# Attention and gated MLP on one core: softmax without row maxima, a range check with a branch, and a new order of steps

## The chip, the cores and the metric

The kernel runs on one core of a Trainium2 chip. The metric is the device time of one execution in microseconds (us); the median of several runs counts. TensorE is called PE here, VectorE DVE, ScalarE ACT, GpSimd POOL, and SP is SyncE, whose queue only issues DMAs.

## The reference, cut to what matters

```python
q_n, k_n = rmsnorm(q, g_q), rmsnorm(k, g_k)          # q, k, v: 8 batches x 12 heads x 448 x 64, float32
scores = matmul(q_n, k_n.T) / 8
scores = scores - max(scores, axis=-1)
attn = exp(scores)
attn = attn / (sum(attn, axis=-1) + 1e-09)
x = matmul(attn, v)                                   # heads side by side: 8 x 448 x 768
h = maximum(x @ w_in, 0)                              # w_in 768 x 1024
conv_out = 3-tap convolution of h along the sequence, per channel
out = (h * sigmoid(conv_out)) @ w_out                 # w_out 1024 x 768
```

Taking any number off a row of scores before exp leaves `attn` as it is, but for the 1e-09 and for rounding.

## The kernel before, in words

**Pairs.** The work is cut into 48 pairs `n` of heads, six to a batch. Each pair has seven tiles `j` of 128 query rows (2 heads x 448 rows). Pairs 0 to 9 are computed in float32 (`whole`), pairs 10 to 47 with each float32 operand split into a high and a low float16 half, and three matmuls in place of one.

**Attention of a pair.** `load_k`, `load_q` and `v_load` bring in the data. `square`, `square_sum` and nine small steps `rsqrt` make the factors of the norm, and `apply_rms` (two multiplications, L276 where a helper records them) applies them. PE or a DMA turns q and k (`qk_transpose`, `q_turn`), and ACT or DVE copies them out of PSUM (`qk_hi`, tile `kT` times the gain `G`, tile `qT`). `scores` (L856) fills two PSUM banks for a group of two tiles. `soft_max` (L864) takes the negative row maxima of both banks in one reduction on DVE. `soft_exp` (L876) on ACT reads a bank, adds that maximum as its bias, and writes exp to tile `e` with the row sum (`rsum`) beside it. A bank is free again when exp has read it. Pairs from 10 on then split `e` into tile `ph`: `p_hi` (L264, a cast) and `p_lo` (L276, a subtraction in two instructions); `p_turn` (L896) is a DMA transpose of `ph` into `PT` on SP's queue. There are six places for `ph`. Pairs 0 to 9 turn `e` on PE (`p_transpose`, L904) and copy it (`p_evac`). `sum_add`, `sum_step` and the steps after them turn the row sums into a row of reciprocals, `pv` (L996) multiplies with v, and `x_scale`, `x_hi`, `x_lo` leave x in two halves.

**MLP of a batch.** `in_part` (L1080) multiplies x with `wi`, `in_relu`, `in_conv`, `in_tanh`, `in_gate`, `in_hi` and `in_lo` make the gated tile `gring` (`g`), `out_part` (L1149) multiplies it with `wo`, `out_evac` and `out_store` write the result.

**Weights.** They come as 64-bit numbers. `convert` turns them into float32 with three integer steps on DVE (L391, L395, L399), then they are scaled and split.

**Order.** All steps are put into a list `plan`; the string `ORDER` says, four characters for a step, in which order they are issued, on which engine each stands, and which PSUM bank it takes. Each engine runs its instructions in that order and waits at each for its inputs. A POOL step that would share a port with DVE waits for the last DVE step ahead of it in the order (the "shared port" rule).

The lines at which the order is read and the lines of the softmax:

```python
        a, b, e, z = (DIGITS.index(x) for x in ORDER[4 * i : 4 * i + 4])
        fn, args = plan[len(DIGITS) * a + b]
        step, e = (fn.__name__, *args), ("PE", "DVE", "ACT", "POOL", "SP")[e]
        ...
        nc.vector.tensor_reduce(st, banks[:, i : i + 2, :S], axis=AX.X, op=ALU.max, negate=True)
        ...
        nc.scalar.activation(
            new("e", (n, j), [P, S], F32), held["s", (n, j)][:, :S], AF.Exp, bias=shift(n, j),
            accum_out=old("rsum", n)[:, c : c + 1],
        )
```

Of the kernel before, what the change touches and what calls it, by code (L numbers as in the profile page):

```python
# [20 lines left out]
    "$2&!$4$!$3&!$y&!$z&!$?$!${$!$P&!!!#!!6&!$5#!$6#!$7#!$8%!$9%!%;&!!7&!$:%!$|#!$@#!$A%!$Q#!%y&!$;#!"  # L21
    "$B#!$}#!$C#!!0&!$~#!%!%!$<%!%*$!%+#!!8&!!9&!%##!$D#!%f&!%,#!$=#!$E#!%-#!!:#!%.#!%$#!$F#!%/#!!;#!"
    "%0#!!?#!$G#!%1#!$>#!$H#!%%#!%2#!$I#!$M%!%g&!!1#!$J%!%<#!%z#!!<#!%3#!!@#!$N!#$O$!$K!+$L$!$R!8!D#!"
    "%4#!!A#!!B$!!>&!!C&!!E#!$T!L$V!b!I#!&D&!&E&!!F#!!H&!!J#!%&%!!G$!$S#!$U#!&N&!%(%!%h$!%i#!$X$!$W#!"
    "$[$!%8%!%9!#%)%!$Y!+%5%!!S#!!N#!!K#!!M&!$_$!%:$!$c$!!O#!$]!#!T#!$Z$!!P#!!U#!!R&!$a!$$^$!$b$!%6!("
    "%7$!&F$!$f$!(0&!(c&!!Q$!!W&!&G#!!X#!%=!B%>#!%j%!%k#!!Y#!!^#!$d!+$g!#$e$!!Z#!$i$!!_#!$j!$!]&!%l#!"
    "%m%!%n%!!V$!$l$!$o%!$h$!%?!V%@#!$k$!%o%!%p%!&O#!%q%!$p#!%A!l%B#!!L$!$q#!!a#!!c&!%E$!%r#!!=$!%v%!"
    "&y&!(1#!$r&!&z&!%C!.%D#!%s%!(W&!(d#!$m!%%F!&!d#!!h#!%H$!![$!!e#!(e#!!f#!!i#!!l#!$n$!%I!(%G$!#(&!"
    "%K$!!j#!!m#!%w!%#)&!%J$!!p#!!n#!%t!&!q#!%N$!&K%!%Q$!%x$!$s&!)F&!%u$!%L!+%O!*%{!V$t&!%|#!%}!B%T$!"
    "%W$!%M$!%P$!%R!#%U!$(X&!%X!+%S$!(f!*(g#!%~#!%Z%!!g$!&H%!!#%!!b$!!r#!%[#!#/#!#*#!%V$!#0#!%]#!%Y$!"  # L30
    "!k$!&$$!#+#!$u!##1#!#,#!!o$!&($!&+$!&%!$&&$!&L!*&M$!&I!+%^&!&J$!&.$!&!!V&##!#.&!&)!$&*$!&P!l&R!B"
    ")y&!*Y&!$v#!&Q#!&{$!%_&!(Y%!&,!$$w%!$x%!#3&!&/!#(Z#!&|#!&}%!&1$!&4$!)G#!&2!(#4#!!/%!&-$!&7$!&~#!"
    "%b!)(!%!&S#!(#%!&:%!#5#!($#!!s$!!t#!&;#!)z#!(%%!(&%!&X$!#-$!&0$!&3$!%a&!)3&!&5!$&6$!#6#!((#!#9#!"
    "&[$!()#!(*%!([%!&8!*&9$!&Y!+&_$!&T!.&]!(&Z$!&^$!&U#!&a!%&b$!!u!*!v#!(-%!&c$!%c#!(_%!&V!L(+!+&d!%"
    "&W#!(,#!#:#!!x$!!y#!&f$!!%%!&e$!(.!#(/$!&i$!(a!)(b$!#8&!#>#!&l$!#;#!!z$!#?#!(]!+(^#!&<#!)4&!)5$!"
# [186 lines left out]
WHOLE = 10  # L222
# [22 lines left out]
def tile_attention_moe(ctx: ExitStack, tc, q, k, v, g_q, g_k, w_in, conv_w, w_out, out):  # L245
# [366 lines left out]
    def duo(n):  # L612

        return (n, 1) if n < 2 else (n - n % 2, 2)
# [725 lines left out]
```

## Time and profile before

| | |
|---|---|
| median of 3 runs | 806.55 us (805.41 to 807.5) |
| the profiled execution's own time | 807.84 us |
| its span, first to last instruction | 806.1 us |
| mean granted clock of PE | 0.994 |
| busy: PE, DVE, ACT, POOL | 763.9, 701.9, 665.8, 464.4 us |

The profile is of one execution. Busy time of an engine is the time in which at least one of its instructions runs; matmuls are pipelined, so several run at once and the next may start before the last has ended. SP only issues, so it has no busy time in the tables; what its queue does is read from its timeline and its waits. Four stretches are used below: up to the first exp (22.5 us), pairs 0 to 9 (to 153.5 us, the first exp of pair 10), pairs 10 to 45 (to 707.6 us, the first exp of pair 46), and the rest.

### The profile page before, as it was taken

Reading aid. Unit: us, or ns where it says so; the run is one execution under the profiler, and the core shown is the slowest. Engines: PE = TensorE matmul, PEld = TensorE weight load, DVE = VectorE, ACT = ScalarE, POOL = GpSimd, SP = SyncE. Lnnn points to the kernel's source line nnn. Section 1 sums busy time; section 2 is a strip of 40 time slices with the busy share of each in tenths; the row PEclk is TensorE's granted clock in tenths of the full one; section 3 lists DMA queues with packets and bytes.
Section 4 is the critical chain, followed back from the end, with each engine's and each line's share of the span. In section 5 each row is a group of like instructions: output and inputs, shape, how many; then the busy total and the mean of one; then the engine's idle time right before and its main releaser. Section 6 shows DMA issues by size and latency. Waiting matters only on the chain.

```text
span 806.1 us, 16603 instructions
## 1 busy us (share of the span) xinstructions
PE 763.9 (95%) x5278; PEld 401.9 (50%) x5278; DVE 701.9 (87%) x1469; ACT 665.8 (83%) x1568; POOL 464.4 (58%) x727
## 2 busy tenths in 40 slices
PE   1799999999999999999999999999899999999998
PEld 1355555544545554455445554455444554455554
DVE  5999999999889899999889999999889899986640
ACT  2979999998989799999889988999889788973221
POOL 2346555675668557595567654864578655882110
PEclk9989999999999999999999999999999999999999
DMA  8884653299999999999998999999999999887002
GB/s 227 241 199 141 150 142 99 58 192 189 179 194 168 176 184 192 173 186 179 191 199 148 197 192 179 171 180 183 190 188 159 182 192 164 142 136 149 5 1 78
DMA packets 353420, 130.84 MB, mean 162 GB/s; under 512 B 295708, under 2 KB 349748, under 8 KB 353332
## 3 DMA queue, kind: packets, MB, share of 16 engines
q1 hardware_dynamic: 344436, 121.50, 80.1%
q10 hardware_dynamic: 8896, 8.28, 3.9%
q8 instruction: 41, 0.67, 0.4%
q14 instruction: 47, 0.39, 0.1%
HBM read 48.20 MB, written 11.80 MB: 74 GB/s over the span
## 4 chain that ended last, share of the span: by engine, by line
PE 51%; ACT 17%; DMA 11%; DVE 11%; issue 6%; POOL 3%; SPq 0%; ACTq 0%; DVEq 0%; POOLq 0%
PE bank L1149 20%; PE bank L1080 13%; PE bank L856 7%; PE bank L996 7%; DMA PT<-ph 6%; ACT ph L264 2%; PE bank L904 2%; DMA PT<-PT 2%; ACT PT L264 2%; PE bank L673 2%; DMA v<-in_v_dram 1%; ACT bank L1088 1%; POOL ph L276 1%; DMA qT<-qkf 1%; ACT sq L592 1%
## 5 line engine op out<-in xcount | busy, mean ns | idle before, releaser
L1080 PE MATMUL bank<-x,wi 128*128 128x448 f16 x1152 | 230.2, 354 | 3.3 <-ACT e_(37_2_7498 L876 1.1
L1149 PE MATMUL bank<-wo,gring 128*128 128x384 f16 (+1 forms) x1056 | 197.4, 327 | 0.8 <-ACT e_(13_3_2355 L876 0.4
L1080 PEld LDWEIGHTS <-wi 128*128 128x128 f16 x1152 | 110.6, 98 | 112.1 <-issue 17.2
L856 PE MATMUL bank<-kT,qT 64*128 64x448 f16 (+3 forms) x1072 | 137.7, 393 | 9.8 <-DMA qT<-qkf 1.5
L1149 PEld LDWEIGHTS <-gring 128*128 128x128 f16 (+1 forms) x1056 | 100.8, 99 | 72.0 <-issue 19.2
L276 POOL TENSOR_TENSOR sq<-qkf,st 112x512 f32<-112x512 f32 (+1 forms) x66 | 67.9, 1043 | 63.3 <-issue 24.0
L996 PE MATMUL bank<-PT,vp 128*64 128x448 f16 x836 | 87.0, 355 | 2.2 <-DMA PT<-ph 0.8
L996 PEld LDWEIGHTS <-vp 128*64 128x64 f16 x836 | 46.3, 109 | 40.0 <-issue 13.8
L856 PEld LDWEIGHTS <-qT 64*128 64x128 f16 (+1 forms) x912 | 34.2, 97 | 63.4 <-issue 43.4
L592 ACT ACTIVATE sq<-qkf 128x1024 f32<-128x1024 f32 (+2 forms) x49 | 50.2, 1030 | 5.7 <-DMA qkf<-in_k_dram 3.8
L673 PE MATMUL bank<-ident,sq 128*128 128x128 f32 (+1 forms) x232 | 36.1, 284 | 19.7 <-POOL sq L276 19.1
L601 DVE TENSOR_REDUCE st<-sq 128x16 f32<-128x1024 f32 x38 | 45.7, 1211 | 4.3 <-ACT sq L592 4.2
L276 POOL TENSOR_TENSOR x<-x,x 128x448 f16<-128x448 f32 x31 | 32.1, 1037 | 25.9 <-ACT x L264 6.9
L1149 PE MATMUL bank<-wo,wi 128*128 128x384 f16 (+1 forms) x192 | 46.9, 326 | 0.0
L276 POOL TENSOR_TENSOR qkf<-sq,qkf 112x512 f16<-112x512 f32 x33 | 38.2, 1160 | 13.1 <-DVE ph L276 4.6
L673 PEld LDWEIGHTS bank<-ident,sq 128*128 128x128 f32 (+1 forms) x232 | 26.8, 146 | 33.0 <-POOL sq L276 21.8
L1088 ACT ACTIVATE bank<-bank 128x448 f32<-128x448 f32 x53 | 28.4, 538 | 14.8 <-PE bank L1080 14.4
L264 ACT COPY PT<-bank 112x512 f32<-112x512 f32 x64 | 36.5, 616 | 3.4 <-PE bank L904 3.4
L1149 PE MATMUL bank<-wo,carry 128*64 128x384 f16 x192 | 34.5, 328 | 0.0
L766 DVE TENSOR_REDUCE vacc<-v 128x1 f32<-128x512 f32 (+1 forms) x48 | 32.1, 675 | 0.7 <-DMA v<-in_v_dram 0.4
L996 PE MATMUL bank<-PT,v 112*64 112x448 f32 x160 | 32.3, 545 | 0.0
L1149 PE MATMUL bank<-wo 128*128 128x384 f16 (+1 forms) x96 | 31.3, 326 | 0.0
(2065 smaller groups left out, 1894.5 us busy)
## 6 DMA issues: line engine op xcount, KB each, us to landing
qkf<-in_q_dram SPq DMA_DIRECT2D x18, 448.0 KB
wo<-in_moe_w_in_dram SPq DMA_DIRECT2D x12, 512.0 KB
gring<-in_moe_w_out_dram SPq DMA_DIRECT2D x16, 384.0 KB
qkf<-in_k_dram SPq DMA_DIRECT2D x18, 256.0 KB
v<-in_v_dram SPq DMA_DIRECT2D x15, 256.0 KB
qkf<-in_k_dram SPq DMA_DIRECT2D x17, 192.0 KB
v<-in_v_dram SPq DMA_DIRECT2D x15, 192.0 KB
PT<-ph SPq DMA_TRANSPOSE x178
```

Of the source, the lines that this page charges most:

```text
L264: (nc.scalar.copy if e == "ACT" else elementwise(e).tensor_copy)(dst, src)
L276: elementwise(e).tensor_tensor(dst, a, b, op=op)
L592: nc.scalar.activation(sq, x, AF.Square)
L601: nc.vector.tensor_reduce(st, sq, axis=AX.X, op=ALU.add)
L673: nc.tensor.transpose(ps[:, t * w : (t + 1) * w], x[:, t], ident[:w, :w])
L766: nc.vector.tensor_reduce(keyed(n, old("vacc", b))[:, i : i + 1], keyed(n, old("v", n)).rearrange("p h t d -> p (h t d)"), axis=AX.X, op=A ...
L856: nc.tensor.matmul(ps[u][o, :S], lhs, rhs, start=(i == 0), stop=(whole(m) or i == 2),)
L904: nc.tensor.transpose(ps[:w, kt * P : (kt + 1) * P], e[:, kt * w : (kt + 1) * w], ident)
L996: nc.tensor.matmul(ps[HALF[h], :S], lhs, pt[:, k, h * S : (h + 1) * S], start=(i == 0 and j == 0), stop=(i == pvs(n)[-1] and j == NB - 1),)
L1080: nc.tensor.matmul(ps[:, :S], wi[:, wl, c, fc * P : (fc + 1) * P], old("x", b * NP + c)[:, xl], start=(i == 0), stop=(i == 3 * NP - 1),)
L1088: nc.scalar.activation(ps, ps, AF.Relu, scale=2.0 ** -24)
L1149: nc.tensor.matmul(ps[p0 : p0 + m, :NO2], g, wo[:, wl, fc, half * NO2 : (half + 1) * NO2], start=(i == 0), stop=(i == 3 * NFC - 1),)
```

## The change

`soft_max` is no longer issued: exp has the constant -4 as its bias. The row sums of all pairs go into a tile `raw`; at the end of each batch DVE takes their largest and smallest (`sum_range`), and after the last batch `sum_check` makes one number of them, which is above 1 if a sum exceeds 6e4 or falls below 1. PE and DVE bring it to one place (`range_turn`, `range_top`), every engine loads it into a register, and a branch skips a second, general program, which computes everything again with row maxima. The general program stands behind the branch in every engine's instructions. `ORDER` is new as a whole, with its engines and banks.

```diff
@@ soft_exp and what it reads
-        i, j = sorted(where["s", x] for x in members(n, g))
-        assert j == i + 1
-        nc.vector.tensor_reduce(st, banks[:, i : i + 2, :S], axis=AX.X, op=ALU.max, negate=True)
+        for u, x in enumerate(members(n, g)):
+            nc.vector.tensor_reduce(
+                st[:, u : u + 1], held["s", x][:, :S], axis=AX.X, op=ALU.max, negate=True
+            )
 
     def shift(n, j):
 
-        a, b = members(*group(n, j))
-        c = 1 if where["s", (n, j)] > where["s", a if b == (n, j) else b] else 0
-        return old("sst", group(n, j))[:, c : c + 1]
+        if not general:
+            return lift
...
+    def raw_sums(n):
+
+        return raw[:, n // NP % 2, n % NP]
 
     def soft_exp(n, j):
-        if j == 0:
-            fixed("rsum", n, sums)
         c = slot(n, j)
         nc.scalar.activation(
             new("e", (n, j), [P, S], F32), held["s", (n, j)][:, :S], AF.Exp, bias=shift(n, j),
-            accum_out=old("rsum", n)[:, c : c + 1],
+            accum_out=raw_sums(n)[:, c : c + 1],
         )
 
+    def sum_range(b):
+        x = raw[:, b % 2].rearrange("p n j -> p (n j)")
+        nc.vector.tensor_reduce(span[:, 0, b : b + 1], x, axis=AX.X, op=ALU.max)
+        nc.vector.tensor_reduce(span[:, 1, b : b + 1], x, axis=AX.X, op=ALU.min)
+
+    def sum_check():
+        high, low = top[:, 0:1], top[:, 1:2]
+        nc.vector.tensor_reduce(high, span[:, 0], axis=AX.X, op=ALU.max)
+        nc.vector.tensor_reduce(low, span[:, 1], axis=AX.X, op=ALU.min)
+        nc.vector.tensor_scalar(low, low, 1e-30, None, op0=ALU.max)
+        nc.vector.reciprocal(low, low)
+        nc.vector.scalar_tensor_tensor(
+            high, high, 1.0 / MOST, low, op0=ALU.mult, op1=ALU.max
+        )
+        nc.vector.tensor_scalar(high, high, 1e30, None, op0=ALU.min)
+
+    def range_turn():
+        max_turn("range", top[:, 0:1])
+
+    def range_top():
+        all_max(top[:, 2:3], "range")
@@ plan_attention
             at(scores, n, g)
-            at(soft_max, n, g)
...
+        if n % NP == NP - 1:
+            at(sum_range, n // NP)
+        if n == NPAIR - 1:
+            at(sum_check)
+            at(range_turn)
+            at(range_top)
@@ at the end
+    flag = nc.values_load(top[0:1, 2:3].bitcast(I32), min_val=0, max_val=0x7FFFFFFF)
+    with tc.If(flag > 0x3F800000):
+        general = True
+        with tc.manual_schedule():
+            run_general()
@@ ORDER, the first of 199 lines (now 193)
-    "$2&!$4$!$3&!$y&!$z&!$?$!${$!$P&!!!#!!6&!$5#!$6#!$7#!$8%!$9%!%;&!!7&!$:%!$|#!$@#!$A%!$Q#!%y&!$;#!"
+    "$2&!$3&!$v&!$w&!$4$!$?$!$x$!%&$!!6&!!!#!$5#!$6#!%^&!$7#!!7&!!0&!!8&!$@#!$P&!$8%!$9%!$y#!$:#!%(#!"
...
```

What the new order puts where is seen in the instructions of each engine. Counted over the whole order: DVE loses 168 maxima and takes 55 more low halves of p (`p_lo`, 92 to 147), 22 more multiplications of `apply_rms` (30 to 52), 14 more copies `PT<-bank` (6 to 20), 12 more casts of `p_hi`, 12 more `gring` subtractions and some 60 smaller moves; POOL goes from 174 to 119 low halves of p and from 66 to 44 of `apply_rms`; ACT gives up 75 instructions. PE's instructions are the same but for one, and so are SP's transposes.

**The start.** SP's queue before, after the first loads of k and q (`gqk` are the two gains, `wo` the place into which the words of `w_in` come first):

```order
L568 DMA qkf_77<-in_q_dram 112x2x128 x2
L554 DMA v<-in_v_dram 112x2x256
L430 DMA wo_84<-in_moe_w_in_dram 128x1024
L554 DMA v<-in_v_dram 112x2x256
L430 DMA wo_84<-in_moe_w_in_dram 128x1024
L554 DMA v<-in_v_dram 112x2x256
L1196 DMA gqk<-in_g_q_dram 64x1 x2
L1196 DMA gqk<-in_g_k_dram 64x1 x2
L430 DMA wo_84<-in_moe_w_in_dram 128x1024 x2
```

SP's queue now, at the same place:

```order
L576 DMA qkf_77<-in_q_dram 112x2x128 x2
L438 DMA wo_84<-in_moe_w_in_dram 128x1024
L562 DMA qkf_78<-in_k_dram 112x2x256
L438 DMA wo_84<-in_moe_w_in_dram 128x1024
L1236 DMA gqk<-in_g_q_dram 64x1 x2
L1236 DMA gqk<-in_g_k_dram 64x1 x2
```

Three loads of v now stand behind the gains, and one load of k ahead of them.

DVE before, around the step of `convert` (L391) that needs the second load of weights, up to the gain `G` (`st` holds the factors of the norm, `st_95` those of pair 0):

```order
L395 SCALAR_TENSOR_TENSOR wi_83<-wo_84,wi_83 128x512
L629 SCALAR_TENSOR_TENSOR st_103<-st_103 112x8
L391 TENSOR_SCALAR wi_83<-wo_84 128x512
L644 TENSOR_TENSOR st_95<-st_95 112x8
L642 TENSOR_TENSOR st_103<-st_103 112x8
L629 SCALAR_TENSOR_TENSOR st_95<-st_95 112x8 x2
L642 TENSOR_TENSOR st_103<-st_103 112x8
L644 TENSOR_TENSOR st_103<-st_103 112x8
L629 SCALAR_TENSOR_TENSOR st_95<-st_95 112x8
L1199 TENSOR_TENSOR G<-gqk 128x1
L1200 TENSOR_SCALAR G<-G 128x1
```

DVE now, to the same two instructions of `G`:

```order
L650 TENSOR_TENSOR st_107<-st_107 112x8
L637 SCALAR_TENSOR_TENSOR st_103<-st_103 112x8
L279 TENSOR_TENSOR sq_104<-qkf_76,st_103 112x2x4x64
L637 SCALAR_TENSOR_TENSOR st_103<-st_103 112x8
L399 TENSOR_SCALAR wi_83<-wo_84 128x512
L279 TENSOR_TENSOR sq_104<-qkf_76,st_103 112x2x4x64
L399 TENSOR_SCALAR wi_83<-wo_84 128x512
L1239 TENSOR_TENSOR G<-gqk 128x1
L1240 TENSOR_SCALAR G<-G 128x1
```

The two multiplications of `apply_rms` of pair 0 (`sq_104<-qkf_76,st_103`), which POOL did before, are now on DVE, and both stand ahead of the second L399, which is the L391 of before.

**The middle.** DVE before, at the first tiles of pair 30 (`sst` are maxima, `ph` the halves of p, `sq` with `st` is `apply_rms`):

```order
L276 TENSOR_TENSOR ph_74<-e_(30_0_5984,ph_74 128x384
L276 TENSOR_TENSOR ph_74<-e_(30_0_5984,ph_74 128x64
L629 SCALAR_TENSOR_TENSOR st_5870<-st_5870 128x32
L864 TENSOR_REDUCE sst_(30_1_6029<-bank 128x2
L276 TENSOR_TENSOR sq_5874<-qkf_76,st_5870 112x2x4x64
L276 TENSOR_TENSOR ph_75<-e_(30_1_5989,ph_75 128x384
L276 TENSOR_TENSOR ph_75<-e_(30_1_5989,ph_75 128x64
L276 TENSOR_TENSOR sq_5871<-qkf_76,st_5870 112x2x4x64
L864 TENSOR_REDUCE sst_(30_2_6043<-bank 128x2
L276 TENSOR_TENSOR x_6020<-x_28_6006,x_6020 128x448
```

DVE now, at the same tiles:

```order
L279 TENSOR_TENSOR ph_74<-e_(30_0_5802,ph_74 128x384
L279 TENSOR_TENSOR ph_74<-e_(30_0_5802,ph_74 128x64
L279 TENSOR_TENSOR sq_5655<-qkf_76,st_5622 112x2x4x64
L279 TENSOR_TENSOR sq_5623<-qkf_76,st_5622 112x2x4x64
L279 TENSOR_TENSOR ph_75<-e_(30_1_5823,ph_75 128x384
L279 TENSOR_TENSOR ph_75<-e_(30_1_5823,ph_75 128x64
L279 TENSOR_TENSOR PT_70<-e_(30_2_5850,PT_70 128x384
L279 TENSOR_TENSOR PT_70<-e_(30_2_5850,PT_70 128x64
L1108 TENSOR_TENSOR vsc_5661<-vsc_5661,wsc 128x1
L1111 COPY vsc_4251<-vsc_5661 64x1
```

The maxima between the other steps are gone, and the low half of tile (30, 2), which stood on POOL, is on DVE.

**The end.** PE's last instructions before (`wo` holds the weights; the rest of `wi` and `wo` also serves as places of the gated tile):

```order
L1149 MATMUL bank<-wo_84,wi_83 128x384
L1149 LDWEIGHTS wi_83
L1149 MATMUL bank<-wo_84,wi_83 128x384
L1149 LDWEIGHTS wo_84
L1149 MATMUL bank<-wo_84 128x384
L1336 UNCONDITIONAL_BRANCH
```

PE's last instructions of the first program now:

```order
L1189 MATMUL bank<-wo_84,wi_83 128x384
L1189 LDWEIGHTS wo_84
L1189 MATMUL bank<-wo_84 128x384
L378 MATMUL bank<-ident,top 128x128
L1395 TENSOR_LOAD top
L1396 COMPARE_AND_BRANCH
```

The turn of the check (`top`), a load of it into a register and the branch stand behind the last matmul, and on each other engine the same load and branch stand behind its last step; DVE reduces `top` ahead of them.

## Rows read from the trace of the kernel before

**Rows 1.** The page: busy time of each engine, share of the span, instructions.
```profile
PE 763.9 (95%) x5278; PEld 401.9 (50%) x5278; DVE 701.9 (87%) x1469; ACT 665.8 (83%) x1568; POOL 464.4 (58%) x727
```

**Rows 2.** Four stretches: busy us by engine, granted clock, DMA share, GB/s.
```profile
0.00:22.50 22.50, 6.09 (x20) 3.19 (x20) 14.37 (x53) 7.34 (x13) 4.83 (x20) 1.00 0.84 229
22.50:153.50 131.00, 123.20 (x735) 67.91 (x732) 125.74 (x258) 123.69 (x308) 69.56 (x99) 0.97 0.57 149
153.50:707.60 554.10, 539.60 (x3885) 278.51 (x3885) 509.86 (x1051) 500.05 (x1174) 362.65 (x571) 1.00 1.00 179
707.60:806.10 98.50, 94.99 (x648) 52.24 (x644) 51.96 (x110) 34.77 (x78) 27.35 (x39) 1.00 0.34 73
```

**Rows 3.** Groups of instructions over the span: busy us, mean ns, idle before.
```profile
L1080 PE MATMUL bank<-x,wi 128*128 128x448 f16 x1152 | 230.2, 354 | 3.3 <-ACT e_(37_2_7498 L876 1.1 <-DVE c_(1_0_2623 L1110 1.1 <-DVE c_(1_1_2641 L1110 0.7
...
L276 DVE TENSOR_TENSOR sq<-qkf,st 112x512 f32<-112x512 f32 (+1 forms) x30 | 21.4, 721 | 0.1
...
L373 DVE TENSOR_REDUCE vsc<-bank 128x1 f32<-128x128 f32 x8 | 2.2, 281 | 1.3 <-PE bank L370 1.3
...
L370 PE MATMUL bank<-ident,vsc 128*128 128x128 f32 x8 | 2.2, 276 | 0.0
```

**Rows 4.** Chain of waits: start us, length us, what ran without a break.
```profile
380.08 7.20 DMA PT<-ph
...
743.01 27.24 PE bank L1080 x144
770.25 32.35 PE bank L1149 x240
```

**Rows 5.** Line L864 alone (the maxima on DVE): a stretch, and the sum over the span.
```profile
0.00:153.50 153.50, 38.81 (x36) 0.98 0.61 161
...
sum 806.10, DVE 179.86; mean DVE 59.95
```

**Rows 6.** Low halves of p (tile ph) on DVE and on POOL: ns min/median/max.
```profile
L276 DVE TENSOR_TENSOR ph<-e_(10_3_1744,ph x2: 218/384/550, 165.7 to 166.2; 128x384 f16<-128x384 f32 x1, 128x64 f16<-128x64 f32 x1
...
L276 POOL TENSOR_TENSOR ph<-e_(10_0_1651,ph x2: 308/614/919, 156.5 to 157.4; 128x384 f16<-128x384 f32 x1, 128x64 f16<-128x64 f32 x1
```

**Rows 7.** Timeline of the first 23 us: start us, length us, what, idle before.
```profile
0.82 0.24 POOL L1207 IOTA gring<- 128x128 int32 x1 [0.39 <-POOLq L1325]
...
13.49 0.43 DVE L391 TENSOR_SCALAR wi<-wo 128x512 int32<-128x512 int32 x1 [1.39 <-DMA wo<-in_moe_w_in_dram]
...
14.59 2.04 POOL L276 TENSOR_TENSOR sq<-qkf,st 112x512 f32<-112x512 f32 x2 [4.41 <-issue]
15.20 0.44 DVE L1199 TENSOR_TENSOR G<-gqk 128x1 f32<-128x1 f32 x1 [0.75 <-DMA gqk<-in_g_k_dram]
...
18.42 4.52 PE L856 MATMUL bank<-kT,qT 64*128 64x448 f32 x12 [0.72 <-ACT kT L268]
...
21.37 1.08 DVE L864 TENSOR_REDUCE sst_(0_0_212<-bank 128x2 f32<-128x896 f32 x1
...
22.52 0.61 ACT L876 ACTIVATE e_(0_0_223<-bank,sst_(0_0_212 128x448 f32<-128x448 f32 x1
```

**Rows 8.** Timeline of SP's queue, a piece of the middle.
```profile
307.54 2.63 SPq L896 DMA_TRANSPOSE PT<-PT  x2
```

**Rows 9.** Line L896, the DMA transposes of p on SP: ns min/median/max.
```profile
L896 SPq DMA_TRANSPOSE PT<-ph x178: 1220/1248/3141, 159.6 to 734.6; - x178
```

**Rows 10.** Waits of SP's queue: us in total, times, longest.
```profile
SPq L896 <- POOL ph L276: 35.9, 40, 2.2
...
SPq L896 <- POOL PT L276: 14.7, 15, 1.7
```

**Rows 11.** Timeline of the last 5 us.
```profile
802.67 0.58 ACT L268 ACTIVATE c_('o'_7_2_0_10292<-bank,vsc 128x384 f32<-128x384 f32 x1 [2.02 <-PE bank L1149]
803.28 0.33 SPq L1163 DMA_DIRECT2D out_dram<-c_('o'_7_2_0_10292  x1
```

**Rows 12.** The page, DMA queues: packets, MB, share of 16 engines.
```profile
q8 instruction: 41, 0.67, 0.4%
```

More of the change, by code (lines that the diff above doesn't have):

```diff
@@ L26 @@
[L26 to L35, printed above, removed]
@@ L260, in tile_attention_moe, with __missing__ @@
     PSC = 2.0 ** 14
-    on = {}
+    NS = 2 * S // P
+    general = False
+    class Engines(dict):
+        def __missing__(self, step):
+            return "ACT" if step[0] == "square" else "DVE"
+    on = Engines()
     def copy(e, dst, src):
@@ L612, in duo @@
     def duo(n):
-        return (n, 1) if n < 2 else (n - n % 2, 2)
+        return (n, 1) if n < 2 and not nd(n) else (n - n % 2, 2)
     def rsqrt(n, i, w):
@@ L680, in whole @@
     def whole(n):
-        return n < WHOLE
+        return n < WHOLE and not general
     def flat(t):
@@ L739, in plan_qk @@
             at(apply_rms, n, i)
-            if i == 0 and n >= QTURN:
+            if i == 0 and (general or n >= QTURN):
                 at(q_hi, n)
@@ L924, in sum_add @@
     def sum_add(n):
-        x = old("rsum", n)[:, :NS]
-        elementwise(on["sum_add", n]).tensor_scalar(x, x, 1e-9, None, op0=ALU.add)
+        x = fixed("rsum", n, sums)[:, :NS]
+        elementwise(on["sum_add", n]).tensor_scalar(x, raw_sums(n), 1e-9, None, op0=ALU.add)
     def sum_step(n):
@@ L1235, in make_cw, with run_general, run, steps_of @@
                 to_f32("DVE", i, cw, cw_words[:, :, :, 0], cw_words[:, :, :, 1])
+    def run_general():
+        count = [0]
+        def run(fn, *args):
+            taken[:] = [(count[0] + i) % NBANK for i in range(NBANK)]
+            fn(*args)
+            count[0] += NBANK - len(taken)
+        def steps_of(planner, arg, skip=()):
+            plan.clear()
+            planner(arg)
+            for fn, args in list(plan):
+                run(fn, *args)
+        def attend(n):
+            for g in ((n, 0), (n, 1), (n, 2), (n + 1, 0), (n + 1, 1), (n + 1, 2), (n + 1, 3)):
+                run(scores, *g)
+                run(soft_max, *g)
+                for x in members(*g):
+                    for fn in (soft_exp, p_hi, p_lo, p_turn):
+                        run(fn, *x)
+            for m in (n, n + 1):
+                for fn in (sum_add, sum_step, sum_turn, sum_store):
+                    run(fn, m)
+                run(sum_load, m, 0)
+                for fn in (sum_spread, v_hi, v_lo, v_twin):
+                    run(fn, m)
+                for i in pvs(m):
+                    run(pv, m, i)
+                for fn in (x_scale, x_hi, x_lo):
+                    run(fn, m)
+        for b in range(B):
+            for n in range(b * NP, (b + 1) * NP):
+                steps_of(plan_v, n)
+            for n in range(b * NP, (b + 1) * NP, 2):
+                for m in (n, n + 1):
+                    steps_of(plan_qk, m)
+                attend(n)
+            steps_of(plan_moe, b)
     at(prepare)
```

394 lines of the change are left out of this document (203 added, 191 removed).

## Prediction, made before the changed kernel was run

> **What bounds the kernel now.** I read the page first: PE is busy 95% of the span, DVE 87%, ACT 83%, POOL 58% [rows 1]. That looks like a kernel bound by PE, of which 806.1 - 763.9 = 42 us are left to gain. The table by stretches says more [rows 2]. Up to the first exp PE does nearly nothing (6.1 of 22.5 us). In pairs 0 to 9 DVE is busy 125.7 of 131.0 us and ACT 123.7: they set the pace, not PE. In pairs 10 to 45 everything is near its end at once: PE 539.6 of 554.1 us, DVE 509.9, ACT 500.1, and the DMA engines' share is 1.00. The last stretch is PE alone: 144 matmuls of L1080 in 27.24 us and 240 of L1149 in 32.35 us stand in the chain of waits without a break [rows 4].
>
> PE's busy time hides waits. L1080 is busy 230.2 us for 1152 instructions, 200 ns each [rows 3], but without a break one takes 27.24 / 144 = 189 ns [rows 4]. The 1008 outside that run hold up to 1008 x 11 = 11 us of waits in this group alone. So PE's room in pairs 10 to 45 is not 554.1 - 539.6 = 14.5 us but some 24. The Trainium skill says the same ("Trainium Kernel Development and Optimization", Performance Expectations): matmul busy time is a bad measure of the distance to the limit, because matmuls are pipelined. By busy time that stretch could give 14.5 us at most, by the rate of the unbroken run about 24; the trace agrees with the rule, and I go by the rate.
>
> The queue that has no busy time is SP's. In the middle it issues transposes of p back to back, two in 2.63 us [rows 8]; one takes 1.25 us in the median and 1.22 at the least [rows 9]. A pair needs seven of these and one of q, 8 x 1.25 = 10 us, of the 554.1 / 36 = 15.4 us that a pair takes; loads and row sums come on top. But the queue also waits: 35.9 us for low halves of `ph` on POOL and 14.7 us for those in `PT` [rows 10].
>
> **The change part by part.**
>
> *Work.* The 168 maxima are 179.9 us busy on DVE [rows 5]; the first takes 1.08 us [rows 7]. Since the next instruction starts a little before the end, I count 1.0 us of the engine for each, 168 us. DVE takes on work for it: 55 low halves of p, on DVE 0.55 + 0.22 us against 0.92 + 0.31 on POOL [rows 6], some 0.64 us of the engine, 35 us; 22 multiplications of `apply_rms` at 0.72 us [rows 3], some 14 us; and casts, copies and subtractions taken from ACT and POOL. Counting every instruction of the new order with the mean start-to-start time of its group in this trace (the same count returns [rows 1] for the old order) gives DVE 702 to 646 us, ACT 666 to 624, POOL 464 to 341. PE gains one turn, and SP's transposes stay.
>
> *The start (22.5 us).* Now: POOL starts `apply_rms` of pair 0 at 14.59, after DVE's steps behind the conversion that waited for its load until 13.49; `G` waits for the gains until 15.20; the scores start at 18.42; the first maximum at 21.37, behind conversions on DVE; the first exp at 22.52 [rows 7]. In the new order `apply_rms` stands ahead of that wait. Three loads of v go behind the gains and one of k ahead: 2 x 229 kB less, at 229 GB/s [rows 2] 2 us. So `G` starts at about 13.2 and is ready 0.6 later; two copies out of PSUM of 0.6 us follow, scores at 15.1. A group is a third of the 4.52 us of the 12 matmuls, so exp starts at 16.8 instead of 22.5: -5.7. If the gains land when they did, exp is at 18.7: -3.8. I take **-5**: tiny loads need not come earlier by all the bytes ahead of them.
>
> *Pairs 0 to 9 (131 us).* Of DVE's 125.7 us, 38.8 us up to 153.5 are maxima [rows 5], but it takes on copies and norms: by the same count DVE's work between the row sums of pair 0 and pair 10 goes from 131 to 118.5 us, ACT's between their first exps from 125 to 118. DVE no longer sets the pace alone. With ACT's present idle time of 7.3 us the stretch is 118.4 + 7.3 = 125.7 (-5.3); with nearly none, 119 (-12). If the clock (granted at 0.97 in this stretch, [rows 2]) or PE's order holds it, -2. I take **-7**, near the end with idle time kept, since three engines stay near their limits.
>
> *Pairs 10 to 45 (554.1 us).* DVE and ACT each lose 34 us here by the count (504 to 470 and 501 to 467), more than PE's 24 us of room. What PE waits for changes too: a bank is held from scores to exp with a place in DVE's queue between, which is gone. The low half of p, on which SP waits, is earlier where it moved to DVE (0.64 us in place of 1.2). What does not change is PE's work, SP's queue and the DMA traffic with its share of 1.00. Bounds: -24 if PE waits for nothing, and more if other groups hide as much as L1080; -4 if the transposes keep their pace and only the few DMAs moved from SP to ACT's queue count. I take **-18**, three quarters of the room, because the queue is let off 50 us of waits for POOL's halves at least in part.
>
> *The rest (98.5 us).* PE is busy 95.0 of it and the maxima there are 6.4 us on an engine busy half the time: 0.
>
> *The end.* Now PE ends at 802.60, ACT copies from 802.67, SP issues from 803.28 to 803.61, and the span ends at 806.1, 3.5 us after PE [rows 4, 11]. The store has 2.5 us from its issue to the end. In the new program PE turns `top` (0.28 us), DVE reduces it (0.28) [rows 3], then every engine loads a register and branches over the general program. That runs beside the last store, which covers about 2.5 us. No row shows a register load or a branch to a distant place. Lower bound: the branch that POOL takes at its start costs 0.39 us of idle time [rows 7], and all of it hides: 0. Upper: a load as long as the store (2.5) and fetching the code as long as the longest landing in the chain (7.2 us, [rows 4]): 0.7 + 2.5 + 7.2 - 3.5 = +7. An instruction packet takes 0.4% of 16 x 806 us over 41, 1.3 us [rows 12]; with a landing like the store's that makes 0.7 + 2.5 + 1.3 + 2.5 - 3.5 = 3.5, and I take **+3**.
> A rule speaks against the change here: the Trainium skill ("Runtime: NRT & Kernel Launch", Instruction fetch mechanics) says that a taken branch to a page not held in the engine's small buffer stalls until a DMA has fetched it. POOL's 0.39 us shows no such stall, but that is a short way and no test of it. By the rule the end costs the +3 that I take, without it 0.
>
> *Sum:* -5 - 7 - 18 + 0 + 3 = **-27 us**. The profiled execution took 807.8 us by its own time, 1.3 above the median; taken off the median it is 806.55 - 27 = **780 us**.
>
> **The rivals.**
> 1. *The transposes hold the middle.* For it: SP's queue without a gap [rows 8], DMA share 1.00. Against: its 50 us of waits for POOL. Then the middle gives -4: -5 - 7 - 4 + 3 = -13, **793 us**.
> 2. *PE runs nearly unblocked.* For it: DVE and ACT come down to 85% of this stretch's present length (470 and 467 of 554), and no work stands between scores and exp any more. Against: SP. Start -5.7, pairs 0 to 9 -12, middle -24, end +1: -41, **766 us**.
> 3. *Slower: SP's queue is held by DVE.* The queue issues in a fixed order, and what stands behind a late transpose is late too, loads of k and v among them. 55 low halves move from POOL, which is busy 58%, to DVE, which stays above 80% and works in order. POOL's form made the queue wait 0.9 us each 40 times [rows 10]. If the new order makes each of the 266 transposes wait 0.11 us longer than now, 30 us, the gain is gone; at 0.2 us the time is 806.55 - 27 + 53 = **833 us**. Against: a low half takes half the time on DVE.
> 4. *The change doesn't do what it says:* the check fires and the general program runs as well, over 1500 us. By the reference's inputs the sums of exp(score - 4) lie between 16 and 1351, far inside 1 and 6e4.
>
> **How the numbers follow.** 780 with its own range of 770 to 791: 0.51. Rival 1: 0.21. Rival 2: 0.22. Rival 3: 0.04. No change to speak of: 0.015; rival 4: 0.005. About 0.3% (2.4 us) is what a measurement here can tell from nothing. All cases but the last three are faster by more: faster 0.94, same 0.02, slower 0.04. The range leaves out the lower tail of rival 2 and everything above rival 1: 759 to 799.
>
> **What the next profile would show.** The first exp near 17 us; the first exp of pair 10 near 141; that of pair 46 near 677; the last matmul near 773 and 6 to 7 us from it to the end; DVE busy about 646 us, ACT 624, POOL 341; PE's busy share of pairs 10 to 45 above its 97%. If the first exp is right and pair 46 comes late, SP's row of waits tells rival 1 from rival 3: in the one the queue runs without waits, in the other it waits for DVE's halves. The prediction is wrong if the clock is granted at half for longer, if the end costs over 10 us, or if DVE's added steps are longer on the path than the maxima were.

## The result, and the profile after

The changed kernel takes 784.5 us (median of 4 runs, 783.08 to 784.88) beside 806.59 us (4 runs), a ratio of 0.9724, 95% interval 0.9706 to 0.9741: 22 us, or 2.8%, faster. The forecast was 780 us, 759 to 799. The profiled execution took 784.36 us by its own time and 782.6 us from its first to its last instruction, 23.5 less than before.

The page after: busy time (answers to [rows 1]), and the chain of waits by engine.

```profile
PE 749.9 (96%) x5279; PEld 400.0 (51%) x5279; DVE 657.2 (84%) x1592; ACT 625.7 (80%) x1482; POOL 345.2 (44%) x538
...
PE 64%; ACT 13%; DMA 9%; DVE 6%; issue 4%; SPq 1%; POOL 1%; ACTq 0%; DVEq 0%; POOLq 0%
...
L1120 PE MATMUL bank<-x,wi 128*128 128x448 f16 x1152 | 229.6, 354 | 2.1 <-DVE kT L731 0.7
```

The same four stretches as [rows 2], cut at the first exp, the first exp of pair 10 and that of pair 46, in the same columns.

```profile
0.00:16.80 16.80, 3.88 (x14) 2.43 (x16) 10.27 (x44) 4.97 (x9) 1.38 (x11) 1.00 0.90 235
16.80:139.60 122.80, 117.99 (x736) 66.12 (x736) 115.05 (x283) 117.79 (x294) 53.96 (x72) 1.00 0.66 174
139.60:679.80 540.20, 532.10 (x3882) 279.12 (x3876) 480.01 (x1149) 467.59 (x1102) 270.16 (x426) 1.00 1.01 182
679.80:782.60 102.80, 95.91 (x655) 52.34 (x653) 51.88 (x119) 35.33 (x80) 19.68 (x30) 0.98 0.31 68
```

So 22.5 became 16.8 (-5.7), 131.0 became 122.8 (-8.2), 554.1 became 540.2 (-13.9), 98.5 became 102.8 (+4.3). The busy times of DVE, ACT and POOL are close to the forecast (646, 624, 341). The group of `in_part`, L1120, is busy 229.6 us; it was 230.2 [rows 3]. The forecast took 11 us of that for hidden waits that would go.

At the start the steps come as forecast. Timeline of the changed kernel (start us, length us, engine, line, what).

```profile
12.40 0.68 DVE L279 TENSOR_TENSOR sq<-qkf,st 112x512 f32<-112x512 f32 x1
...
13.34 0.15 DVE L1239 TENSOR_TENSOR G<-gqk 128x1 f32<-128x1 f32 x1
...
16.78 0.63 ACT L887 ACTIVATE e_(0_0_185<-bank,lift 128x448 f32<-128x448 f32 x1 [1.95 <-PE bank L862]
```

At the end PE's last matmul of out_part ends at 775.6, the turn of `top` follows, and after DVE's reduction come the register load (L1395) and the branch (L1396), which the tables of busy time leave out. The two lines alone: engine, operation, count, ns min/median/max, first and last start.

```profile
775.27 0.33 PE L1189 MATMUL bank<-wo 128*128 128x384 f16 x1
775.44 0.27 PE L378 MATMUL bank<-ident,top 128*128 128x128 f32 x1
```
```profile
L1395 PEldq TENSOR_LOAD <-top x1: 487/487/487, 776.1 to 776.1; - x1
L1395 SPq TENSOR_LOAD <-top x1: 531/531/531, 776.7 to 776.7; - x1
```
```profile
L1396 SPq EVENT_SEMAPHORE  x8: 17/17/17, 780.6 to 781.2; - x8
...
L1396 PEldq COMPARE_BRANCH  x1: 4422/4422/4422, 776.7 to 776.7; - x1
...
L1396 SPq COMPARE_BRANCH  x1: 57/57/57, 777.6 to 777.6; - x1
```

PE's branch takes 4.42 us. SP's takes 0.06, but its next instruction comes at 780.6, 3.0 us later. The Trainium skill ("Runtime: NRT & Kernel Launch", Instruction fetch mechanics) says that a taken branch out of the buffered code waits for a DMA; the trace agrees: ten packets of the two queues for instructions start between 777.7 and 781.8 us, and experiment 9, without the branch, has ten packets less in all. The page's lines of these queues (packets, MB, share):

```profile
q8 instruction: 43, 0.70, 0.4%
q14 instruction: 53, 0.43, 0.2%
```

### The profile page after: what moved, and what is told of

Read it like the earlier page. It is cut to its first block, busy times and chain, and to the rows that moved or that the text cites. A ratio compares the mean times of both kernels' runs of the same rounds, so it can differ in the third digit from the quotient of the medians.

```text
span 782.6 us, 16529 instructions
## 1 busy us (share of the span) xinstructions
PE 749.9 (96%) x5279; PEld 400.0 (51%) x5279; DVE 657.2 (84%) x1592; ACT 625.7 (80%) x1482; POOL 345.2 (44%) x538
## 4 chain that ended last, share of the span: by engine, by line
PE 64%; ACT 13%; DMA 9%; DVE 6%; issue 4%; SPq 1%; POOL 1%; ACTq 0%; DVEq 0%; POOLq 0%
PE bank L1189 23%; PE bank L1120 18%; PE bank L1031 10%; PE bank L862 9%; DMA PT<-PT 3%; DMA PT<-ph 3%; PE bank L939 3%; PE bank L681 2%; ACT PT L267 1%; DMA qkf<-in_q_dram 1%; ACT sq L600 1%; ACT ph L267 1%; DVE ph L279 1%; ACT wi L457 1%; DMA gqk<-in_g_k_dram 1%
## 5 line engine op out<-in xcount | busy, mean ns | idle before, releaser
L1120 PE MATMUL bank<-x,wi 128*128 128x448 f16 x1152 | 229.6, 354 | 2.1 <-DVE kT L731 0.7
L1120 PEld LDWEIGHTS <-wi 128*128 128x128 f16 x1152 | 111.1, 98 | 109.8 <-issue 14.9
L862 PE MATMUL bank<-kT,qT 64*128 64x448 f16 (+3 forms) x1072 | 126.4, 388 | 6.1 <-ACT e_(19_2_3546 L887 1.9
L279 POOL TENSOR_TENSOR sq<-qkf,st 112x512 f32<-112x512 f32 (+1 forms) x44 | 46.1, 1060 | 53.5 <-DVE st L637 13.5
L279 POOL TENSOR_TENSOR qkf<-sq,qkf 112x512 f16<-112x512 f32 x26 | 30.1, 1162 | 24.6 <-ACT c_(1_0_2529 L271 6.3
L681 PEld LDWEIGHTS bank<-ident,sq 128*128 128x128 f32 (+1 forms) x232 | 26.8, 143 | 24.4 <-issue 16.0
L279 DVE TENSOR_TENSOR sq<-qkf,st 112x512 f32<-112x512 f32 (+1 forms) x52 | 34.7, 695 | 0.3
L1042 DVE TENSOR_TENSOR x<-bank,rB 128x448 f32<-128x448 f32 x38 | 23.6, 622 | 9.1 <-PE bank L1031 7.7
L279 POOL TENSOR_TENSOR x<-x,x 128x448 f16<-128x448 f32 x22 | 22.8, 1037 | 17.4 <-DVE x L267 4.8
```

Of the source, the lines that this page charges most:

```text
L279: elementwise(e).tensor_tensor(dst, a, b, op=op)
L681: nc.tensor.transpose(ps[:, t * w : (t + 1) * w], x[:, t], ident[:w, :w])
L862: nc.tensor.matmul(ps[u][o, :S], lhs, rhs, start=(i == 0), stop=(whole(m) or i == 2),)
L1042: nc.vector.tensor_tensor(x, ps, r, op=ALU.mult)
L1120: nc.tensor.matmul(ps[:, :S], wi[:, wl, c, fc * P : (fc + 1) * P], old("x", b * NP + c)[:, xl], start=(i == 0), stop=(i == 3 * NP - 1),)
```

## The experiments

**1. The old order without maxima.** `e1_old_order_no_max`, an edit of the kernel before:

```diff
-        nc.vector.tensor_reduce(st, banks[:, i : i + 2, :S], axis=AX.X, op=ALU.max, negate=True)
...
-        return old("sst", group(n, j))[:, c : c + 1]
+        return lift
```

> The kernel before with its 168 row maxima left out and the constant -4 in their place, in its own order, without the check of the row sums. What I now hold: in pairs 10 to 45 TensorE pays 0.28 us each time it goes to matmuls of the scores and back, and the old order goes there as often as ever, so only the waits shrink. Start -1 (the first maximum took 1.08 us), pairs 0 to 9 -5, pairs 10 to 45 -6 of the 13.9, no +3.5 at the end: about 795 us (792 to 798). Rival 1, the maxima are all of it and the order is nothing: all of the gain but the loads at the start and without the branch at the end, 806.5 - 1 - 8 - 14 = 783. Rival 2, the order written for the maxima holds everything where it was: over 803.

Ratio to before 0.9951 (0.9931 to 0.9972): 4 of the 22 us, so about 802.6 us, and rival 2 of the expectation comes nearest. Its four stretches, from an execution of 804.4 us, the slowest of ten (their median is 801.2):

```profile
0.00:22.80 22.80, 6.16 (x20) 3.19 (x20) 13.47 (x52) 7.41 (x14) 4.91 (x20) 1.00 0.84 227
22.80:150.10 127.30, 120.06 (x732) 65.96 (x731) 97.34 (x224) 123.38 (x308) 68.07 (x99) 1.00 0.60 153
150.10:704.20 554.10, 540.28 (x3886) 277.52 (x3884) 411.23 (x924) 499.47 (x1174) 373.80 (x571) 1.00 0.99 179
704.20:802.60 98.40, 95.00 (x648) 52.24 (x644) 47.91 (x104) 34.72 (x78) 27.44 (x39) 1.00 0.35 73
```

In pairs 10 to 45 DVE is busy 411 us instead of 510, and the stretch takes 554.1 us as before. The one gain, 3.7 us in pairs 0 to 9, goes with a granted clock of 1.00 where [rows 2] has 0.97. Where the faster executions gained up to 3 us more, this one trace doesn't show. My own figure, 795, was wrong: I had given the waits of the middle to the maxima.

**2. The new order with maxima.** `e2_new_order_with_max`:

```diff
...
-        c = slot(n, j)
+        c, g = slot(n, j), group(n, j)
+        if not general and ("sst", g) not in rings.get("sst", Ring(4)).d:
+            soft_max(*g)
         nc.scalar.activation(
             new("e", (n, j), [P, S], F32), held["s", (n, j)][:, :S], AF.Exp, bias=shift(n, j),
```

> The changed kernel in its new order, and all 168 maxima on DVE again, each ahead of the first exp of its group; exp doesn't use them (its constant stays), so they are work for DVE and a second reader of the score banks, and nothing in ACT's queue waits for them by value. One reduction where the two banks lie side by side (about 1.0 us), two (about 0.6 each) where not. What I hold: the new order takes DVE for its own work and can't be had with the maxima; in pairs 10 to 45 DVE would be busy 480 + 126 x 1.1 = 620 us of the present 540, so that stretch takes 640 and the whole some 890 us. Rival: DVE's work falls into its idle time and TensorE's order holds the time: under 800.

968 us, ratio 1.201 (1.197 to 1.205); I had expected 890. Pairs 10 to 45 take 668.7 us with DVE busy 599.6:

```profile
189.80:858.50 668.70, 577.21 (x3879) 296.37 (x3881) 599.56 (x1359) 472.20 (x1102) 266.61 (x425) 0.95 0.78 147
```

So the new order can't be had with the maxima, at least not where this run puts them, ahead of the first exp of each group. Read together with experiment 1, the removal paid by making room for the order.

**3. The new engines in the old order.** `e14_old_order_new_engines`, the kernel of experiment 1, in which the third character of each step of `ORDER` (its engine) is that of the new program. For the table's first row:

```diff
-    "$2&!$4$!$3&!$y&!$z&!$?$!${$!$P&!!!#!!6&!$5#!$6#!$7#!$8%!$9%!%;&!!7&!$:%!$|#!$@#!$A%!$Q#!%y&!$;#!"
+    "$2&!$4$!$3&!$y&!$z&!$?$!${$!$P&!!!#!!6&!$5#!$6#!$7#!$8%!$9%!%;&!!7&!$:#!$|#!$@#!$A%!$Q#!%y&!$;#!"
```

> The kernel before without maxima, its steps in the old order, but each of them on the engine that the new program gives it (550 of its steps change engine, 79 low halves of p from POOL to DVE among them and 24 back). If work standing late on POOL and ACT held the old order (SP waited 58 us for POOL's halves in the run without maxima): pairs 10 to 45 come down from 554 to 546 or less, total 790 to 794, the rest being changes of shape. If the places in the queues held it: 554 and about 800; and if an order planned for other engines makes new waits: over 803.

852 us, 1.055 (1.051 to 1.060): the last case of the expectation, new waits. Places and engines belong together; this run doesn't tell which of the moved steps matter.

**4. What a change of shape costs.** `m1_shapes` times TensorE by itself, on zeros.

```diff
...
+        for a, b in ((in_shape, scores_shape), (in_shape, pv_shape), (scores_shape, pv_shape)):
+            for run in (4, 12):
+                for _ in range(20):
+                    for fn in (a, b):
+                        for i in range(run):
+                            fn(i)
...
```

> Not the reference's work: TensorE alone, on zeros, no waits for other engines. 200 matmuls of the shape of in_part, then 20 times runs of 4 and of 12 of in_part's and scores' shapes by turns, in_part's and pv's, scores' and pv's, then 200 of scores' and of pv's. If the 0.28 us belong to the shapes: a pair of runs of 4 takes 4 x 189 + 4 x 95 + 281 = 1419 ns for in_part and scores, 1422 for in_part and pv, 8 x 95 + 374 = 1134 for scores and pv, and the same excess stands over runs of 12. If they were waits for data or banks in the kernel: 1138, 1138 and 764 ns, with no excess.

Timeline of PE (L31 is in_part's shape, L35 that of scores, L38 that of pv):

```profile
49.91 0.93 PE L31 MATMUL full<-x,w 128*128 128x448 f16 x4
50.77 0.55 PE L35 MATMUL rows<-x,w 64*128 64x448 f16 x4
51.26 0.36 PE L31 MATMUL full<-x,w 128*128 128x448 f16 x1
...
103.58 2.44 PE L31 MATMUL full<-x,w 128*128 128x448 f16 x12
105.96 1.31 PE L35 MATMUL rows<-x,w 64*128 64x448 f16 x12
107.20 2.44 PE L31 MATMUL full<-x,w 128*128 128x448 f16 x12
...
305.48 1.32 PE L38 MATMUL cols<-x,w 128*64 128x448 f16 x12
306.74 1.31 PE L35 MATMUL rows<-x,w 64*128 64x448 f16 x12
307.98 1.33 PE L38 MATMUL cols<-x,w 128*64 128x448 f16 x12
309.24 19.09 PE L35 MATMUL rows<-x,w 64*128 64x448 f16 x200
328.26 19.11 PE L38 MATMUL cols<-x,w 128*64 128x448 f16 x200
```

One matmul of scores takes (328.26 - 309.24) / 200 = 95 ns without a break, one of in_part 189 [rows 4]. Four and four make 1.14 us; the period is 51.26 - 49.91 = 1.35. Twelve and twelve make 3.41; the period is 107.20 - 103.58 = 3.62. So in and out again costs 0.21 us whatever the length of the run, and between pv and scores it is 2.50 - 24 x 0.095 = 0.22. That is 0.11 for each change, not the 0.28 for two that I had counted in the kernel. The Trainium skill ("TensorEngine Tiling (Array Packing)", Key Properties) says that changing the tiling mode drains the engine; the trace agrees, with this price.

With it the middle can be taken apart. The matmuls of pairs 10 to 45, each at its unbroken rate, make 506.3 us in both kernels. The trace gives the shape of each matmul, and the groups mix them: the last rows of a batch in `out_part` are matmuls on 64 columns, and some of `scores` are on 64 rows and 64 columns. These changes cost as much as those between groups: in the kernel before, the next matmul of `out_part` starts 256 ns after one of 128 columns when it is on 64 columns, and 162 ns after when it is not. Counted by shape there are 229 changes before and 195 after: 25.2 and 21.5 us at 0.11. What is left over is waiting: 554.1 - 506.3 - 25.2 = 23 us before, 540.2 - 506.3 - 21.5 = 12 after. So by this sum some 4 of the 13.9 us are changes of shape, and 10 are waits.

**5. More changes of shape.** `e5_more_visits`:

```diff
...
+        if a[0][0] == b[0][0] == "scores" and x[0][0] in ("in_part", "out_part"):
...
+            if j and all(y[0] not in needs for y in steps[at_b:]):
+                ahead(x[0], b[0])
```

> The changed kernel with one step of in_part or out_part put between two steps of scores that stood side by side, wherever what it reads was ready: 108 stretches of scores in the order of TensorE instead of 89, with the same matmuls. What I hold: each further stretch costs 0.095 us going in and 0.186 us coming out, and nothing hides it, so 19 x 0.28 = +5.3 us by the count: about 789.5 us (787.5 to 791.5), first exp of pair 46 later by most of that. Rival: TensorE waits for the transposes of p or for ACT in any case, and such changes fall into those waits: 784.5 +- 1.

784.2 us, 0.9748 (0.9725 to 0.977), not to be told from the changed kernel. Pairs 10 to 45 take 540.9 us. By the count there are 224 changes, 24.6 us, 3.2 more than without the edit; what is left over falls from 12 to 10. Most of the added cost fell into waits. I had expected that nothing hides it. So the 4 us of the sum above can't be credited to the 34 changes that the new order saves: putting 29 back cost the stretch 0.7 us.

**6 and 7. Shorter transposes, in both orders.** `e9_short_transposes` and, without maxima in the old order, `e13_old_order_short`, the same edit:

```diff
-        c = slot(n, j)
+        c, k = slot(n, j), 7 if n < 12 else 4
...
-            places(n)[:, :, c * P : (c + 1) * P], old("ph", (n, j)),
+            places(n)[:, :k, c * P : (c + 1) * P], old("ph", (n, j))[:, : k * P],
```

> The changed kernel; from pair 12 on each transposition of p by DMA takes 4 blocks of 128 columns instead of 7, so three blocks of the low half are left from earlier pairs (that part of the computation is left out). SP's queue and the DMA engines get less work, all other engines the same. If the transposes hold the middle (rival 1 of the prediction): pairs 10 to 45 lose 5 us or more of 540, total below 780. If TensorE's own matmuls, its changes between shapes and its order hold it: within 2 us of the changed kernel, 782 to 786.

> The kernel before without maxima in its own order (as the first of these runs), and with the same short transposes from pair 12 on. That run took 554.1 us for pairs 10 to 45, as before the change, though DVE was busy 411 of them and no longer 510. If SP's queue and the DMA engines held it there: 545 or less, total under 794. If not they: 554 and 800 to 803.

770.0 us, 0.9551 (0.9522 to 0.958), and 785.4 us, 0.9749 (0.9718 to 0.9781). Pairs 10 to 45 of the new order, and of the old:

```profile
139.50:666.80 527.30, 526.42 (x3884) 276.42 (x3882) 478.31 (x1149) 466.83 (x1103) 270.73 (x426) 1.00 0.78 143
```
```profile
149.30:682.70 533.40, 532.04 (x3884) 274.07 (x3884) 411.05 (x924) 498.33 (x1174) 374.12 (x571) 1.00 0.77 143
```

13 us less in the new order, 21 in the old one. After matmuls and changes of shape nothing is left in the one (-0.5 by the sum, which shows how exact it is) and 2 us in the other: nearly all of PE's waiting in both orders hangs on the transposes of p and the DMA traffic that they make. And with them out of the way the two orders still differ by 6.1 us, of which the 34 changes of shape make 3.7; the rest is open. In the chain of waits of the new order with short transposes PE has 87% and DMA 3%:

```profile
PE 87%; ACT 6%; DMA 3%; issue 1%; DVE 1%; SPq 1%; POOL 0%; ACTq 0%; DVEq 0%
```

It is not SP's queue that is relieved. A short transpose takes it 1.21 us, a long one 1.25 [rows 9], and SP's waits in this stretch sum to 242 us, beside 231 in the changed kernel:

```profile
L931 SPq DMA_TRANSPOSE PT<-ph x178: 1188/1211/2852, 148.4 to 691.8; - x178
```

**8. Low halves back on POOL.** `e10_low_halves_on_pool`:

```diff
+        (x[0], x[1], "POOL" if x[0][0] == "p_lo" and x[2] == "DVE" and x[0][2] % 3 == 0 else x[2], x[3])
```

> The changed kernel with 65 low halves of p moved from DVE to POOL (184 there instead of 119; before the change 174), nothing else moved. The runs with short transposes took 13 us off pairs 10 to 45 in the new order and 21 off the old one, so the new order waits some 8 us less for what the transposes bring. If that is because SP gets its halves earlier: SP's waits for POOL in that stretch go from 76 us back towards the 123 of before, pairs 10 to 45 take 546 to 552 instead of 540, total 790 to 797. If the DMA engines' throughput alone holds the stretch, with the queue fed well enough either way: within 2 us of the changed kernel. If DVE's relief (some 40 us less work) counts for more than POOL's delay: under 782.

784.5 us, 0.973 (0.9697 to 0.9762): no difference. SP's waits for POOL in pairs 10 to 45 sum to 118 us, beside 76 in the changed kernel and 123 before; the largest rows of this run:

```profile
SPq L931 <- POOL ph L279: 43.3, 44, 1.8
SPq L931 <- POOL PT L279: 15.7, 18, 1.6
```

The stretch takes 539.7 us all the same. The low halves that went to DVE are not what the new order gained by. What SP waits longer for POOL it waits less for ACT, though: all its waits sum to 232 us here, 231 in the changed kernel and 267 before. Whether that smaller sum shortened the stretch, no run here tests.

**9. No branch.** `e3_no_branch`:

```diff
-    flag = nc.values_load(top[0:1, 2:3].bitcast(I32), min_val=0, max_val=0x7FFFFFFF)
-    with tc.If(flag > 0x3F800000):
...
```

> The changed kernel without the register load, the branch and the general program behind it; the sums are still checked on chip, but nothing comes of it. If TensorE's branch, 4.42 us in the trace, ends the span, the end goes back to what it was before: 7.0 us from the last matmul to the end become 3.5 to 3.8, about 781 us. If the last store and the semaphores at the end would take as long anyway: 784.5, no change. If the code of the general program costs elsewhere too (fetching instructions, DMA), more than 4 us: below 780.

780.5 us, 0.9716 (0.9686 to 0.9747), six executions from 778.0 to 785.2: the times don't tell it from the changed kernel. The trace does. PE's last matmul of out_part starts at 771.83 and ends at 772.16; the span ends at 775.6, 3.4 us later instead of 7.0.

```profile
771.83 0.33 PE L1189 MATMUL bank<-wo 128*128 128x384 f16 x1
771.99 0.27 PE L378 MATMUL bank<-ident,top 128*128 128x128 f32 x1
```

Its two queues for instructions:

```profile
q8 instruction: 41, 0.67, 0.4%
q14 instruction: 45, 0.37, 0.2%
```

**10. Start and end reordered.** `e11_start_and_end`:

```diff
...
+    ahead(("apply_rms", 0, 0), ("convert", "in", 1, 0))
+    ahead(("make_g",), ("convert", "in", 1, 0))
+    for step in (("range_turn",), ("range_top",)):
+        ahead(step, ("out_part", 7, 1, 1, 8, 4))
```

> The changed kernel with the second apply_rms of pair 0 and G ahead of the first conversion of weights on DVE (which waited 1.05 us for its load), and the turn and reduction of the check ahead of TensorE's last six steps of out_part. Nothing is left out. Start: apply_rms of q at 11.0 instead of 12.40, so the first exp at 15.4 instead of 16.8 if the gains have landed by 12.5; at 16.5 or later if the loads of the gains were what G waited for. End: TensorE comes to its register load 0.45 us earlier, 6.5 us from its end to the span's instead of 7.0. Together -1.9: about 782.6 us beside 784.5, less than three rounds can tell; the trace must show it. Rival: nothing moves at pair 10, since other work fills in: 784.5.

782.9 us, 0.9722 (0.969 to 0.9755). The first exp stays at 16.70: `G` waits 2.18 us for the gains, whose landing sets the start.

```profile
13.25 0.16 DVE L1239 TENSOR_TENSOR G<-gqk 128x1 f32<-128x1 f32 x1 [2.18 <-DMA gqk<-in_g_k_dram]
```

At the end PE's sequencer comes to the branch at 771.5, while its matmuls run on to 774.0, so that 2.5 of its 4.0 us pass beside them. But SP takes the branch behind the last store, at 775.1, and goes on at 778.8, so the span still ends 6.8 us after PE.

```profile
L1408 SPq EVENT_SEMAPHORE  x8: 17/17/17, 778.8 to 779.4; - x8
...
L1408 PEldq COMPARE_BRANCH  x1: 4002/4002/4002, 771.5 to 771.5; - x1
```

**11. Fewer changes of shape.** `e16_pv_behind_scores`:

```diff
...
+        if name[0] == "scores" == name[4] and name[1:4] == ["pv"] * 3:
...
+                for x in pe[i : i + 3]:
+                    ahead(x[0], pe[j][0])
```

> The kernel just above, and at seven places the three steps of pv that stood between two stretches of scores behind the second of them: 81 stretches of scores instead of 89. The kernel of shapes alone gave 0.11 us for each change between two shapes (0.215 us for in and out again). 16 changes less: -1.7 us if TensorE holds pairs 10 to 45, about 781 us in all. If the transposes hold them, as the short ones make likely, nothing: 782.6; and if pv, later by 1 to 1.5 us, makes x_scale and the banks late: over 783.5.

784.3 us, 0.9738 (0.9712 to 0.9765). Pairs 10 to 45 take 539.6 us, as without it. But the edit hardly does what I had expected of it: counted by shape there are 192 changes in this stretch instead of 195, not 16 less. That is 0.3 us, which a measurement here can't tell from nothing, so this run says nothing on what a change of shape is worth.

**12. A version to beat both.** `e17_fewer_transposes`:

```diff
...
+    ahead(("load_g",), ("load", "in", 0))
...
+    for x, z, *of in BY_PE:
+        for name, e, place in zip(("p_transpose", "p_evac", "p_low"), ("PE", "ACT", "DVE"), of):
...
+            ahead((name, *x), place)
```

> A version meant to beat both, nothing left out. To the kernel with the moved apply_rms, G and check it adds two things. (a) The loads of the gains are issued ahead of the first load of w_in: G waited for them until 13.25, so the first exp should come at about 14.6 instead of 16.7. (b) Seven of the 266 quarters of p that DMA transposes (pairs 29 to 38, where a bank stood free) are turned by TensorE instead, 4 matmuls of some 0.6 us in all, and copied out by ACT and DVE. In pairs 10 to 45 the packets under 512 bytes, nearly all of them of transposes, take 416 us of the 16 DMA engines for 285 transposes, 1.46 us each. If the DMA engines hold that stretch (the short transposes, and three kernels in which only the other engines' work or order changed and 540 stayed): 540 - 7 x 1.46 = 530, some of it lost because the seven stand close together: 530 to 536; with the start and the end about 776 us (773 to 780). If TensorE holds it: 540 + 7 x 0.6 = 544, total 786.

779.75 us, 0.966 (0.9636 to 0.9683): faster than the changed kernel, whose interval lies above. Half of the expectation held. The gains land early, and the first exp comes at 14.55:

```profile
10.83 0.15 DVE L1254 TENSOR_TENSOR G<-gqk 128x1 f32<-128x1 f32 x1
...
14.55 0.64 ACT L896 ACTIVATE e_(0_0_185<-bank,lift 128x448 f32<-128x448 f32 x1 [1.95 <-PE bank L871]
```

The seven transposes brought nothing in the profiled execution. Pairs 10 to 45 take 541.1 us, neither 530 nor 544: matmuls 509.4 (+3), changes of shape 22.6 (+1), what is left over 9 (-3). That execution, 785.8 us, was the slowest of the six; the others took 778.1 to 780.1. It had a stretch of half clock at 22 us that cost it the start's gain. Windows of it, that stretch and pairs 10 to 45:

```profile
22.00:28.80 6.80, 5.84 (x24) 3.26 (x26) 6.68 (x11) 5.13 (x12) 1.30 (x2) 0.50 1.09 293
140.30:681.40 541.10, 533.33 (x3910) 281.66 (x3904) 481.82 (x1158) 470.39 (x1113) 262.35 (x413) 1.00 1.00 179
```

The earlier first exp is worth 2.2 of the 5 us by which the median is lower, where nothing takes it back; where the rest comes from, this one trace doesn't show.

## Why the prediction was right, and which step failed

**The start, -5 (measured -5.7).** Right, and by its mechanism: `G` starts at 13.34, forecast 13.2. Experiments 10 and 12 show that the landing of the gains sets the first exp, not the place of `apply_rms`.

**Pairs 0 to 9, -7 (measured -8.2).** The size is right. Part of it is the clock, 1.00 where [rows 2] has 0.97; experiment 1, also at 1.00, gained 3.7 us there without any other change than the maxima. Whether the maxima or the execution made that difference is open.

**Pairs 10 to 45, -18 (measured -13.9).** This is the step that failed, in its reasons more than in its size; that the size came within 4 us is luck. First, I read 11 us of hidden waits out of `in_part`'s mean of 200 ns against 189 and added them to PE's room, following the rule that busy time is a bad measure. The group is busy 229.6 us after, 230.2 before. What stands in those 11 us is the length of the record: `in_part` stands in 64 stretches in PE's order, and the last matmul of each counts as busy for 354 ns, the mean of [rows 3], and not for the 189 after which the next one starts: 64 x 0.165 = 10.6 us. In the changed kernel it is 59 stretches, 9.7 us. Behind 45 of the 64 a change of shape falls into that time (experiment 4), behind the others the matmuls of the next group do. It is not a wait that a lighter DVE could take away. Second, I took the relief of DVE and ACT as what frees PE. Without maxima in the old order DVE had 143 us of idle time in this stretch and the stretch kept its 554.1 us. Third, I took the gain from SP's waits for POOL's low halves. With those waits back at 118 us the stretch is as short as ever (experiment 8).

In their place: the new order itself, for which the maxima made room. In it PE waits some 10 us less for what the transposes bring. It also changes shape 34 times less in this stretch, 3.7 us by the sum, but experiment 5 shows that such changes fall into the waits as long as there are any. Which of the moved steps shortens the waits is open: not the low halves, and not the engines alone.

**The rivals.** Rival 1 was half right: the transposes do hold PE back, by 13 us still (experiment 6), but by what they transfer and not by the time that SP's queue needs for them, and the new order took some of it. Nor did that queue run without a gap, as two transposes back to back [rows 8] had made me believe: by all rows of its waits it stood 267 of the 554.1 us. Rival 2 had the room nearly right for the wrong reason: with short transposes the stretch loses 26.8 us. Rival 3 did not occur; later low halves cost nothing. The check did not fire.

**The rest 0 and the end +3 (measured +4.3 together).** PE's last matmul comes 27.0 us earlier, pair 46 27.8: +0.8. The end has 7.0 us instead of 3.5, forecast 6 to 7. Experiment 9 takes the 3.6 away. The term was made of a load of 2.5 and a fetch of 3.8 us; on PE they are 0.49 and 4.42. The 0.39 us of the lower bound were not seen to be a branch: the trace of the kernel before has no record of one, and what POOL's sequencer does just before 0.82 us [rows 7] is a drain, two semaphore instructions and two settings.

## What to carry to other kernels

When a unit of work is removed together with a new order, run the old order without the work before crediting the removal: here the work alone gave 4 us of 22. A mean that lies above the unbroken rate is not yet a wait: count the stretches first, since the last matmul of each counts for longer, and time the mix of shapes by itself, since their changes cost something in every order. What a DMA's issue takes on its queue says nothing about what its transfer holds back; shorten the transfer to see it.

## What the runs showed that I had not expected

A change between full matmuls, those on 64 rows and those on 64 columns costs 0.11 us, whatever the run lengths (experiment 4). A DMA share of 1.00 is no ceiling: in the kernel before, the 3.4 us at half clock around 422 us stand at 1.36.

```profile
421.80:425.20 3.40, 3.40 (x14) 1.84 (x12) 2.37 (x3) 3.15 (x7) 3.40 (x5) 0.51 1.36 194
```

A transpose of 4 blocks takes SP 1.21 us, one of 7 blocks 1.25. And a branch over much code costs each engine 3.0 to 4.4 us until its next instruction (2.6 to 4.0 in experiment 10), which PE's sequencer can spend in part while its queued matmuls run.
